# Attention and a gated MLP on one core: a score block split off, an eviction moved from ScalarE to VectorE, longer exponentials in the planner, new due times

## The chip, the cores and the metric

The kernel runs on one core of a Trainium2 chip. The metric is the device time of one execution in microseconds (us). The kernel before took 622.55 us, the median of three runs (621.22 to 623.7). The engines are named as in the profile: PE is TensorE's matmul stream and PEld its weight loads, DVE is VectorE, ACT is ScalarE, POOL is GpSimd, and SP is the queue that issues every DMA of this kernel.

## The reference, cut to what matters

```
q, k, v: (4, 12, 448, 64)                  # batch, heads, sequence, head size
scores = q @ k.T / 8, causal mask          # 448 x 448 a head
attn   = exp(scores - rowmax); attn /= sum(attn) + 1e-9
x      = (attn @ v), heads side by side    # (1792, 768)
gate   = 1 / (1 + exp(-(x @ w_gate)))      # 768 -> 1536
val    = x @ w_val
out    = (gate * val) @ w_out              # (1792, 768), float32
```

All inputs and the output are float32; the weights arrive in a packed 64-bit form.

## The kernel before, in words

The 48 heads are worked on as 24 pairs, two heads beside each other on the 128 partitions (six pairs for each of the four batch items). The six pairs of batch item 0 are the opening, and nothing but attention can run there at first, since the MLP needs their result. From then on the MLP of earlier batch items fills PE while the attention of later ones goes on beside it.

For one pair of the opening, the score rows are cut in four blocks of 128, 256, 384 and 448 keys (the last one has 64 rows and holds both heads together). `score` puts the products of blocks 0 and 1 in one step, block 2 in a second and block 3 in a third; blocks 0 and 1 of a head share a PSUM buffer. `softmax` then issues, block by block, a VectorE instruction that adds the mask, scales, and keeps the row's minimum of the negated scores (line 410); a ScalarE exponential with a running sum (line 417); two small VectorE instructions for the reciprocal (lines 426, 428); and GpSimd multiplications (line 438). `trans` turns the result on PE in four groups of four 128 x 128 tiles (line 313), and `empty` copies each group out of PSUM, on ScalarE for the groups listed in `EV` (line 322) and on VectorE for the others (line 324). `pv` multiplies with the values (lines 337, 342). From pair 6 on ("wide" pairs) the transposes are made on VectorE and through DRAM instead: `shift` writes the tile `tb` to DRAM as `pd` (line 461) and reads it back in four quarters as `pt` (line 464), and `wpv` (line 481) needs all four and the values `vr` (line 285).

The scores' inputs `raw` (line 274) and an extra piece in `sm` (line 279) are loaded for every pair; pair 0's `raw` comes in two pieces. The packed weights come in as `room` (line 559), are unpacked by ScalarE (line 563) and VectorE (lines 565, 567), stored as `wdram` for later use (line 570), and split in a high and a low part (lines 575, 577), so that each float32 product is three matmuls (lines 594, 807).

The order in which the instructions are written out is not the order of the Python calls. `Plan` notes each piece of work as an operation with an engine, an estimated cost, what it reads and writes, and a due time; operations are numbered as they are noted. `order` works the due times back from consumers to producers (consumer's due time less its cost, less a slack, less an extra of some operations, which for DMA loads is their latency), adds `NUDGE[number]` to single operations, and then plays the engines forward: each engine takes, of the operations that are ready, the one with the earliest due time. The instructions are written out in the order of these planned starts, and each engine and the SP queue then work strictly in that order; on the chip only semaphores hold an instruction back. A load must also follow the load before it in the same ring of buffers. The estimated cost of an exponential of n elements is `act(n, 0, 1) + 0.01`, which is n/1200 + 0.20 us.

Operation numbers that the prediction speaks of, as they count in the changed kernel: 40 is the `raw` load of pair 1, 41 its `sm` piece and 42 the values of pair 0; 253 and 261 are the loads of the first two packed weights (252 and 260 before); 814 is the `pd` store and 815 the first `pt` quarter for the wide pair whose value products come at 162.59 us; 820 to 842 are parts of the softmax of the next wide pair, 883 a GpSimd instruction of the MLP (line 624), 908 that pair's values, and 929 the store of an output tile (line 641). The base due times named there are those that the planner works out for the kernel before, ahead of `NUDGE`.

Of the kernel before, what the change touches and what calls it, by code (L numbers as in the profile page):

```python
# [20 lines left out]
NB = 4  # L21
# [14 lines left out]
AHEAD = 3  # L36
EARLY = 2
WC = 512
EV = (1, 3)
BUFS = dict(w64=3, wd=2, wr=3, ws=3, sm=4, raw=3, pt=2, gt=5, vr=2, st=4, tb=1)  # L40
LAT, LOOK, SLACK = 0.04, 0.06, 0.2
AFTER = dict(DVE=0.09, ACT=0.1, PL=0.03)
# [3 lines left out]
REBIAS, SIGN = 2.0 ** -112, 2.0 ** 32  # L46

NUDGE = {
# [7 lines left out]
}  # L56


# [149 lines left out]
def kernel(  # L208
# [7 lines left out]
    nc = tc.nc  # L216
    plan = Plan()
# [9 lines left out]
    act = lambda n, psum=0, acc=0: n / 1200 + (0.06 if psum else 0.09) + 0.1 * acc  # L227
# [3 lines left out]
    mask = new("mask", [128, ZM + WQ + HALF], F32)  # L231
# [56 lines left out]
    def score(n, blocks, due):  # L288

        j = pairs[n]  # L290
        if blocks[0] == 0:
            for k in ("mn", "sum", "r"):
                j[k] = new(k, [128, 2, NB], F32, BUFS["st"])
            j["sp"] = {}
        tag = "m" if j["b"] == 0 and blocks[0] == 2 and j["k"] < 3 else "s"
        sp = [new(tag, [128, 512], F32, 3, PSUM) for z in range(2)]
        j["sp"].update({i: (sp, woff(i) - woff(blocks[0])) for i in blocks})
        needs = [(j["raw"], *((0,) if blocks[-1] == 1 else (0, 1)))] + ([(j["sm"][1], "x")] if blocks[-1] == 3 else [])
        burst((qk_cost(blocks), lambda: products(j, blocks), needs, [(p,) for p in sp]), due)
        return lambda: softmax(j, blocks)  # L300

    def trans(n, g, due):
# [16 lines left out]
    def empty(j, g, tp):  # L319
        pt, o = j["pt"], 4 * WQ * g  # L320
        if g in EV:
            plan.op("ACT", act(4 * WQ, 1), lambda: nc.scalar.copy(pt.t[:, o:o + 4 * WQ], tp.t), [(tp,)], [(pt, g)])
# [37 lines left out]
    qk_cost = lambda blocks: sum(keys(i) / 600 if i < 3 else 0.4 for i in blocks) + 0.19  # L360
# [28 lines left out]
    def wscore(n, due):  # L389
        j = pairs[n]  # L390
        for k in ("mn", "sum", "r"):
            j[k] = new(k, [128, 2, NB], F32, BUFS["st"])
        a, b = ([new(tag, [128, 512], F32, bufs, PSUM) for z in range(2)] for tag, bufs in (("s", 3), ("t", 2)))
        j["sp"] = {0: (a, 384), 1: (b, 0), 2: (a, 0), 3: (b, 256)}
        burst((1.95, lambda: products(j, range(NB)), [(j["raw"], 0, 1), (j["sm"][1], "x")], [(p,) for p in a + b]), due)
        return lambda: softmax(j, range(NB))

    def softmax(j, blocks):
        mn, su, r_ = j["mn"], j["sum"], j["r"]
        for i in blocks:  # L400
            last = i == 3
            heads = range(1 if last else 2)
            sp, o = j["sp"][i]
            ne, off = keys(i), woff(i)
            for z in range(2):
                sm, n = j["sm"][0 if last else z], HALF if last else ne
                f, lo = (off + HALF * z, (ZM + WQ) * z) if last else (off, ZM - i * WQ)
                to = 1 - z if last else z
                first = lambda z=z, i=i, last=last: mn.t[:, 1, i:i + 1] if last and z else 3.0e38
                plan.op("DVE", dve(n), lambda z=z, i=i, sp=sp, sm=sm, n=n, o=o, f=f, lo=lo, to=to, first=first: nc.vector.tensor_tensor_reduce(  # L410
                    out=sm.t[:, f:f + n], in0=sp[z].t[:, o:o + n], in1=mask.t[:, lo:lo + n], scale=-0.125, scalar=first(),
                    op0=ALU.add, op1=ALU.min, accum_out=mn.t[:, to, i:i + 1],
                ), [(sp[z],), (mask, "end") if last and z else (mask,)] + ([(mn, (1, i))] if last and z else []),
                    [(sm, (i, z) if last else i), (mn, (to, i))])
            for z in heads:
                sm = j["sm"][z]
                plan.op("ACT", act(ne, 0, 1) + 0.01, lambda z=z, sm=sm, i=i, ne=ne, off=off: nc.scalar.activation(  # L417
                    out=sm.t[:, off:off + ne], in_=sm.t[:, off:off + ne], func=ACTF.Exp, scale=-1.0,
                    bias=mn.t[:, z, i:i + 1], accum_out=su.t[:, z, i:i + 1],
                ), [(mn, (z, i))], [*([(sm, (i, 0), (i, 1))] if last else []), (sm, i), (su, (z, i))], extra=0.1)  # L420
            if i < 2:
                continue
            group = (3,) if last else (0, 1, 2)
            a = slice(group[0], group[-1] + 1)
            h = slice(0, len(heads))
            plan.op("DVE", 0.13, lambda h=h, a=a: nc.vector.tensor_scalar_add(r_.t[:, h, a], su.t[:, h, a], 1e-9),
                    [(su, *[(z, e) for z in heads for e in group])], [(r_, last)])
            plan.op("DVE", 0.11, lambda h=h, a=a: nc.vector.reciprocal(r_.t[:, h, a], r_.t[:, h, a]), [], [(r_, last)])  # L428
            for z in heads:
                sm = j["sm"][z]  # L430
                for e in group:
                    o, w = woff(e), keys(e)
                    if j["b"] == 0 and j["k"] == HP - 1 and e % 2:
                        plan.op("ACT", act(w) + 0.1, lambda sm=sm, e=e, o=o, w=w, z=z: nc.scalar.activation(
                            out=sm.t[:, o:o + w], in_=sm.t[:, o:o + w], func=ACTF.Copy, scale=r_.t[:, z, e:e + 1]),
                            [(r_, last)], [(sm, e)])
                    else:
                        plan.op("PL", 0.24 + w / 1200, lambda sm=sm, e=e, o=o, w=w, z=z: nc.gpsimd.tensor_scalar(  # L438
                            out=sm.t[:, o:o + w], in0=sm.t[:, o:o + w], scalar1=r_.t[:, z, e:e + 1], scalar2=1.0,
                            op0=ALU.mult, op1=ALU.mult), [(r_, last)], [(sm, e)])  # L440
# [48 lines left out]
    def burst(part, due):  # L489
        held.append(part)  # L490
# [519 lines left out]
    last = [PAIR * HP + k for k in range(HP)] + [(PAIR + 1) * HP + k for i in range(KH) for k in (i, KH + i)]  # L1010
# [84 lines left out]
```

## Time and profile before

| what | before |
|---|---|
| median of three runs | 622.55 us |
| the profiled execution's own time | 620.8 us |
| its span, first to last instruction | 619.1 us |
| PE busy | 606.9 us (98%) |
| DVE busy | 439.7 us (71%) |
| ACT busy | 335.6 us (54%) |
| POOL busy | 310.6 us (50%) |

Busy time of an engine counts its own instructions; matmuls overlap in the array, so a busy PE is a PE that was never empty and not one at its peak. The profiled execution took 1.75 us less than the median of the runs; the sums are made against its own time.

### The profile page before, as it was taken

The numbers are of one execution on the slowest core, as the hardware profiler recorded it, in microseconds if no ns is written. First come the engines' busy times: TensorE is split into PE (matmuls) and PEld (weight loads), VectorE is DVE, ScalarE is ACT, GpSimd is POOL, SyncE is SP. The second block draws the span as 40 slices with busy tenths as digits, with TensorE's granted clock in tenths as the row PEclk, the third lists the DMA queues.
The fourth block names the chain that finished last, engine by engine and source line by source line (L and its number), as shares of the span: only waits on it lengthen the run. The fifth ranks groups of instructions, "written<-read, shape, count | busy, mean of one in ns | idle before, by whom it ended". The sixth has DMA issues, their size and how long they took to land.

```text
span 619.1 us, 11867 instructions
## 1 busy us (share of the span) xinstructions
PE 606.9 (98%) x4182; PEld 531.5 (86%) x4182; DVE 439.7 (71%) x1048; ACT 335.6 (54%) x754; POOL 310.6 (50%) x350
## 2 busy tenths in 40 slices
PE   6999999999999999999999999999999999999997
PEld 3578888898888888888888899989999989999996
DVE  5897999889855546544648766577754688999752
ACT  6996765675634755555558644434333443657420
POOL 5650534614300676767676676658664666611200
PEclk9999999999999999999999999999999999999999
DMA  8688999998999999878786886855533213534321
GB/s 299 203 308 314 344 370 378 376 397 320 364 396 339 321 365 344 293 245 319 269 323 247 281 311 238 276 199 189 179 110 95 77 52 103 159 117 142 112 75 60
DMA packets 54348, 153.35 MB, mean 248 GB/s; under 512 B 6032, under 2 KB 12432, under 8 KB 51984
## 3 DMA queue, kind: packets, MB, share of 16 engines
q1 hardware_dynamic: 54288, 152.59, 69.6%
q8 instruction: 33, 0.54, 0.3%
q14 instruction: 27, 0.22, 0.1%
HBM read 109.31 MB, written 43.25 MB: 246 GB/s over the span
## 4 chain that ended last, share of the span: by engine, by line
PE 89%; DMA 4%; DVE 3%; ACT 2%; issue 1%; POOL 0%; SPq 0%; DVEq 0%; ACTq 0%; POOLq 0%
PE m L594 39%; PE m L807 19%; PE s L807 10%; PE t L807 7%; PE m L481 5%; PE s L387 4%; PE t L387 2%; DMA raw<-in_qkt_dram 2%; DMA pd<-tb 1%; DMA vr<-in_vt_dram 1%; PE t L313 1%; ACT sm L417 1%; DVE wr L567 1%; DVE sm L410 1%; POOL sm L438 0%
## 5 line engine op out<-in xcount | busy, mean ns | idle before, releaser
L761 POOL TENSOR_TENSOR wl<-room,wh 128x384 fp32r<-128x384 f32 x84 | 98.0, 1190 | 56.0 <-ACT wh L760 56.0
L438 POOL TENSOR_SCALAR sm<-sm,r 128x384 f32<-128x384 f32 (+3 forms) x165 | 94.1, 591 | 63.6 <-DVE r L428 50.2
L594 PE MATMUL m<-xh,wh 128*128 128x448 f32 x288 | 107.3, 372 | 0.0
L594 PE MATMUL m<-xh,wl 128*128 128x448 f32 x288 | 105.3, 366 | 0.0
L594 PE MATMUL m<-xl,wh 128*128 128x448 f32 x288 | 105.2, 365 | 0.0
L417 ACT ACTIVATE sm<-sm,mn 128x384 f32<-128x384 f32 (+3 forms) x168 | 87.6, 524 | 18.6 <-DVE mn L410 15.2
L577 POOL TENSOR_TENSOR wl<-wr,wh 128x768 fp32r<-128x768 f32 x38 | 70.6, 1872 | 24.1 <-ACT wh L575 20.8
L575 ACT CAST wh<-wr 128x768 fp32r<-128x768 f32 x72 | 59.8, 832 | 33.4 <-DVE wr L567 15.0
L760 ACT CAST wh<-room 128x384 fp32r<-128x384 f32 x84 | 39.8, 511 | 52.5 <-PE s L807 12.7
L410 DVE CUSTOM_DVE_ANT_0 sm<-s,mask 128x128 f32<-128x128 f32 (+3 forms) x108 | 42.5, 408 | 25.8 <-PE s L387 25.7
L594 PEld LDWEIGHTS m<-xh,wh 128*128 128x128 f32 x288 | 54.1, 188 | 6.6 <-issue 1.6
L594 PEld LDWEIGHTS m<-xh,wl 128*128 128x128 f32 x288 | 54.1, 188 | 4.5
L594 PEld LDWEIGHTS m<-xl,wh 128*128 128x128 f32 x288 | 54.1, 188 | 4.1
L594 PE MATMUL m<-gh,wh 128*128 128x448 f32 x144 | 53.3, 370 | 0.0
L594 PE MATMUL m<-gh,wl 128*128 128x448 f32 x144 | 52.6, 365 | 0.0
L594 PE MATMUL m<-gl,wh 128*128 128x448 f32 x144 | 52.6, 365 | 0.0
L624 POOL TENSOR_TENSOR gl<-gt,gh 128x448 fp32r<-128x448 f32 x24 | 28.9, 1208 | 37.4 <-ACT gh L623 27.3
L807 PE MATMUL m<-pt,wh 128*128 128x448 f32 x150 | 44.8, 367 | 0.2 <-DVE xl L676 0.2
L453 DVE STREAM_TRANSPOSE room<-sm 128x384 f32<-128x384 f32 (+2 forms) x84 | 35.4, 449 | 8.8 <-POOL sm L438 8.4
L387 PE MATMUL s<-raw 64*64 64x128 f32 (+3 forms) x432 | 35.7, 390 | 4.6 <-DMA raw<-in_qkt_dram 3.5
L481 PEld LDWEIGHTS m<-pt,vr 128*64 128x64 f32 x720 | 33.5, 137 | 7.8 <-issue 4.3
L577 DVE TENSOR_TENSOR wl<-wr,wh 128x768 fp32r<-128x768 f32 x34 | 33.5, 984 | 7.9 <-ACT wh L575 7.4
(177 smaller groups left out, 1373.7 us busy)
## 6 DMA issues: line engine op xcount, KB each, us to landing
room<-in_wp_dram SPq DMA_DIRECT2D x36, 768.0 KB, 7.4
pt<-pd SPq DMA_DIRECT2D x72, 256.0 KB, 5.6
wr<-wdram SPq DMA_DIRECT2D x45, 384.0 KB, 4.6
room<-wdram SPq DMA_DIRECT2D x45, 384.0 KB, 3.6
wdram<-wr SPq DMA_DIRECT2D x36, 384.0 KB, 7.6
pd<-room SPq DMA_DIRECT2D x12, 1024.0 KB, 4.7
raw<-in_qkt_dram SPq DMA_DIRECT2D x23, 448.0 KB, 5.9
vr<-in_vt_dram SPq DMA_DIRECT2D x24, 256.0 KB, 5.3
```

Source lines behind the costliest of these rows:

```text
L387: nc.tensor.matmul(out=sp[z].t[c:c + 64, o:o + ne], lhsT=q, rhs=k)
L410: plan.op("DVE", dve(n), lambda z=z, i=i, sp=sp, sm=sm, n=n, o=o, f=f, lo=lo, to=to, first=first: nc.vector.tensor_tensor_reduce(out=sm.t[ ...
L417: plan.op("ACT", act(ne, 0, 1) + 0.01, lambda z=z, sm=sm, i=i, ne=ne, off=off: nc.scalar.activation(out=sm.t[:, off:off + ne], in_=sm.t[:, ...
L438: plan.op("PL", 0.24 + w / 1200, lambda sm=sm, e=e, o=o, w=w, z=z: nc.gpsimd.tensor_scalar(out=sm.t[:, o:o + w], in0=sm.t[:, o:o + w], sca ...
L453: plan.op("DVE", dve(128 * c) + 0.03, lambda sm=sm, i=i, o=o, c=c, at=at: nc.vector.transpose(out=tv()[:, :, at:at + 32 * c].rearrange("p ...
L481: nc.tensor.matmul(out=vp.t[64 * z:64 * z + 64, i * WQ:i * WQ + rows(i)], lhsT=v.t[:, c, z], rhs=src, start=(c == 0), stop=(c == i))
L575: plan.op("ACT", act(768), lambda: nc.scalar.copy(hi_.t, t.t), [(t,)], [(hi_,)])
L577: plan.op(eng, cost, lambda: at.tensor_tensor(out=lo_.t, in0=t.t, in1=hi_.t.bitcast(F32), op=ALU.subtract), [(t,), (hi_,)], [(lo_,)], lock ...
L594: nc.tensor.matmul(out=ps.t[:, :S], lhsT=a.t[:, k, :], rhs=b.t if isinstance(b, Buf) else b(), start=(first and z == 0), stop=(last and z ...
L760: plan.op("ACT", act(w), lambda: nc.scalar.copy(f(hi_.t), x()), [(src, at)], [(hi_, e)])
L761: plan.op("PL", 0.97, lambda: nc.gpsimd.tensor_tensor(out=f(lo_.t), in0=x(), in1=f(hi_.t).bitcast(F32), op=ALU.subtract), [(src, at), (hi_ ...
L807: nc.tensor.matmul(out=ps.t[:, :S], lhsT=a.t[:, kw, :], rhs=b.at, start=bool(first and z == 0), stop=bool(last and z == 2), skip_group_che ...
```

## The change

Five things change. `EV` loses group 3, so the last of the four transposed groups of each opening pair is copied out of PSUM by VectorE and no longer by ScalarE. In `score`, for the first pair alone (n < 1), the step of blocks 0 and 1 becomes two steps, and block 0 is due 0.3 us ahead of block 1. The dependency of `softmax` on the products is now noted by block instead of by buffer. The planner's cost of an exponential rises by 0.08 us. And `NUDGE` is replaced as a whole; since the first pair has one operation more, all operation numbers from 11 on mean the operation that had a number one lower before.

```diff
-EV = (1, 3)
+EV = (1,)
 NUDGE = {
-    12: -0.9, 31: -3.1, 100: -1.6, 108: -1.6, 144: -3.4, 180: 2.5, 181: 2.5, 187: -3.1, 252: -9.6, 260: -9.6,
...
-    808: 3.4, 811: 3.4, 813: 3.3, 822: -0.2, 835: 0.7, 836: 0.7, 837: 0.7, 838: 9.1, 840: 2, 907: -0.9,
-    928: -8.4, 957: -2.6, 984: 3.2, 1055: -3.7, 1064: -2.4, 1065: -2.4, 1072: 0.5, 1076: -2.4, 1077: -2.4,
...
+    40: 5.9, 49: -4.4, 151: -6.3, 156: -4.1, 157: -4.1, 159: 8.5, 166: 4.9, 263: 2.8, 282: -1.9, 316: 1.7,
...
+    469: -0.5, 472: 13.1, 508: 1.1, 525: -4.3, 648: 4.5, 652: 5, 695: 1.1, 701: -0.7, 815: 3, 820: -16.2,
+    823: -4.7, 826: -4.7, 827: -4.7, 830: -4.7, 831: -4.7, 842: -4.7, 883: 2.1, 921: 1.6, 929: 18, 934: -1.6,
...
 }
...
-        burst((qk_cost(blocks), lambda: products(j, blocks), needs, [(p,) for p in sp]), due)
+        if n < 1 and len(blocks) > 1:
+            for i in blocks[:-1]:
+                plan.op("PE", qk_cost((i,)), lambda i=i: products(j, (i,)), needs, [(p, i) for p in sp], due - 0.3)
+        here = blocks[-1:] if n < 1 else blocks
+        burst((qk_cost(here), lambda: products(j, here), needs, [(p, *here) for p in sp]), due)
...
-                ), [(sp[z],), (mask, "end") if last and z else (mask,)] + ([(mn, (1, i))] if last and z else []),
+                ), [(sp[z], i), (mask, "end") if last and z else (mask,)] + ([(mn, (1, i))] if last and z else []),
...
-                plan.op("ACT", act(ne, 0, 1) + 0.01, lambda z=z, sm=sm, i=i, ne=ne, off=off: nc.scalar.activation(
+                plan.op("ACT", act(ne, 0, 1) + 0.09, lambda z=z, sm=sm, i=i, ne=ne, off=off: nc.scalar.activation(
```

## Rows read from the trace of the kernel before

**Rows 1.** The page's first part: busy us, share of the span, instructions.
```profile
PE 606.9 (98%) x4182; PEld 531.5 (86%) x4182; DVE 439.7 (71%) x1048; ACT 335.6 (54%) x754; POOL 310.6 (50%) x350
```

**Rows 2.** Waits of PE, whole span: us in total, times, longest us.
```profile
PE s L387 <- DMA raw<-in_qkt_dram: 3.5, 1, 3.5
PE m L481 <- DMA vr<-in_vt_dram: 1.8, 2, 1.2
PE t L313 <- POOL sm L438: 0.7, 1, 0.7
PE s L387 <- DVE mn L410: 0.6, 1, 0.6
PE s L387 <- DVE r L426: 0.5, 1, 0.5
PE m L387 <- DMA raw<-in_qkt_dram: 0.5, 1, 0.5
PE t L313 <- DVE pt L324: 0.3, 1, 0.3
PE m L807 <- DVE xl L676: 0.2, 1, 0.2
```

**Rows 3.** Stages: us, then busy us (instructions) of each engine, PEclk, DMA share, GB/s.
```profile
5.00:47.00 42.00, 38.99 (x411) 25.75 (x404) 37.76 (x147) 38.44 (x111) 24.77 (x41) 1.00 0.82 284
...
150.00:200.00 50.00, 48.21 (x318) 43.57 (x320) 34.23 (x61) 25.21 (x42) 5.68 (x11) 1.00 1.01 372
200.00:604.00 404.00, 403.73 (x2594) 361.79 (x2587) 272.07 (x612) 202.11 (x456) 236.93 (x236) 1.00 0.61 209
604.00:619.10 15.10, 11.44 (x57) 10.26 (x55) 3.52 (x6) 0.84 (x1) 0.00 (x0) 1.00 0.17 61
```

**Rows 4.** Timeline of the start: start us, us, instruction [idle before, releaser].
```profile
3.47 1.56 PE L387 MATMUL s<-raw 64*64 64x128 f32 x16 [3.47 <-DMA raw<-in_qkt_dram]
...
5.20 0.29 DVE L410 CUSTOM_DVE_ANT_0 sm<-s,mask 128x128 f32<-128x128 f32 x1 [5.20 <-PE s L387]
```

**Rows 5.** Timeline of the SP queue, first 7 us: when each DMA is issued.
```profile
2.18 0.43 SPq L274 DMA_DIRECT2D raw<-in_qkt_dram  x1
2.66 0.43 SPq L279 DMA_DIRECT2D sm<-in_qkt_dram  x1
3.13 0.43 SPq L285 DMA_DIRECT2D vr<-in_vt_dram  x1
...
4.08 1.15 SPq L559 DMA_DIRECT2D room<-in_wp_dram  x2
...
6.87 3.74 SPq L274 DMA_DIRECT2D raw<-in_qkt_dram  x2
```

**Rows 6.** DMA issues of those windows: KB each, us from issue to landing.
```profile
raw<-in_qkt_dram SPq DMA_DIRECT2D x1, 448.0 KB, 5.1
sm<-in_qkt_dram SPq DMA_DIRECT2D x1, 144.0 KB, 5.0
vr<-in_vt_dram SPq DMA_DIRECT2D x1, 256.0 KB, 5.5
```

**Rows 7.** The two copies of the opening, 5 to 41 us: ns min/median/max.
```profile
L322 ACT COPY pt<-t x9: 562/567/610, 13.4 to 40.0; 128x512 f32<-128x512 f32 x9
L324 DVE COPY pt<-t x9: 674/687/693, 11.7 to 38.2; 128x512 f32<-128x512 f32 x9
```

**Rows 8.** Timeline of ACT: two exponentials that follow each other.
```profile
29.59 0.39 ACT L417 ACTIVATE sm<-sm,mn 128x128 f32<-128x128 f32 x1
29.98 0.39 ACT L417 ACTIVATE sm<-sm,mn 128x128 f32<-128x128 f32 x1
```

**Rows 9.** Timelines of SP, ACT and POOL, 145 to 159 us.
```profile
145.34 0.36 SPq L461 DMA_DIRECT2D pd<-tb  x1
...
157.90 0.89 ACT L563 ACTIVATE wd<-room 128x768 f32<-128x768 f32 x1
...
157.08 1.61 POOL L624 TENSOR_TENSOR gl<-gt,gh 128x448 fp32r<-128x448 f32 x1 [3.62 <-ACT gh L623]
```

More of the change, by code (lines that the diff above doesn't have):

```diff
@@ L394, in wscore @@
         j["sp"] = {0: (a, 384), 1: (b, 0), 2: (a, 0), 3: (b, 256)}
-        burst((1.95, lambda: products(j, range(NB)), [(j["raw"], 0, 1), (j["sm"][1], "x")], [(p,) for p in a + b]), due)
+        burst((1.95, lambda: products(j, range(NB)), [(j["raw"], 0, 1), (j["sm"][1], "x")], [(p, 0, 2) for p in a] + [(p, 1, 3) for p in b]), due)
         return lambda: softmax(j, range(NB))
```

8 rows, old and new, of the table NUDGE are left out of this document.

## The prediction, written before the changed kernel was run

> **What bounds the kernel now.** The page's first part comes first: PE is busy for 606.9 of 619.1 us and no other engine for more than 439.7 [rows 1]. The number and shapes of the matmuls do not change, so the change can only act on the 12.2 us in which PE was empty. The waits of PE say where these lie: 3.5 us until the first input, two waits of together 1.8 us for the values of wide pairs, and then six of 0.7 us and less, five of them in the opening [rows 2]. The windows by stage confirm it: from 200 to 604 us PE lacks 404.00 - 403.73 = 0.27 us, from 150 to 200 us it lacks 1.79, and in the opening, from 5 to 47 us, it lacks 42.00 - 38.99 = 3.01; the 3.66 that it lacks after 604 us are the last output's way out, which the change leaves alone [rows 3]. The reader should take two things from these rows. A speed-up of more than about 1% is not there to be had, and the two places that count are the opening and the two waits near 162 and 180 us. The opening is also the one stage where PE is not alone: ACT is busy for 38.44 and DVE for 37.76 of the 42 us [rows 3], so that all three are above 89%.
>
> Half a per cent, 3.1 us, is about what a measurement of this kernel can tell from no change. That is more than the whole idle time of PE in the opening.
>
> **The change, part by part.** The sum is made against the profiled execution, 620.8 us; the median of the runs is 1.75 us above it, and I add that at the end.
>
> *The split of the first score block: 0 us, between -1.0 and 0.* Before, the 16 matmuls of blocks 0 and 1 run from 3.47 to 5.03 us and DVE starts on block 0 at 5.20, 0.17 after the last of them [rows 4]. Block 1 has twice the columns of block 0, so about two thirds of the 1.56 us are block 1's, and if block 0 alone released DVE, it would start some 1.0 us earlier and all that follows with it. That is the -1.0. I take 0, since the planner lets block 1 start the moment block 0 ends (PE has nothing else then) and plans DVE's first instruction 0.04 us later (its `LAT`), so both product steps are still written out ahead of the read, and both write one PSUM buffer. The trace has a wait for the end of both; it does not say whether the wait goes by the buffer or by the columns.
> The Trainium skill (PSUM — Partial Sum Buffer, section "PSUM bank collisions raise a hardware error") has the rule that semaphores should guard PSUM by bank and quadrant and not by address, as a read beside a write in other columns of the bank already collides. By that rule the read of block 0 has to wait for block 1 and the split is worth nothing; by columns it would be worth the 1.0 us. The trace's 5.20 us agrees with the rule, but a single step would look like this either way.
>
> *The `raw` load of pair 1 goes back: +0.6 us, between 0 and +1.4.* Operation 40 has a base due time of 2.8 and gets +5.9, so 8.7. The `sm` piece (5.1) and the values of pair 0 (6.4) are earlier and now go ahead of it on SP; pair 2's `raw` (8.3) cannot, as it must follow 40 in its ring. The landings give the price: the three were issued at 2.18, 2.66 and 3.13 us [rows 5] and took 5.1, 5.0 and 5.5 us [rows 6], so they landed at 7.3, 7.7 and 8.6. They land one after the other. With `raw` as the last of the three, it lands at about 8.6 and not at 7.3: 1.4 us, rounded with what the issue costs. PE waited for it already (0.5 us, its only wait for `raw` after the first [rows 2]), so that wait becomes 1.9. But behind it PE waited 0.5 us for a DVE instruction and then for GpSimd's multiplications of pair 0, which this load doesn't delay [rows 2]; these waits shrink as PE comes later. If they swallow the delay it costs nothing, if ACT's stream simply starts 1.4 later it costs 1.4. I take a bit under half. In the same move the two 768 KB weight loads lose their -9.6; they were issued at 4.08, ahead of a `raw` that was issued at 6.87 [rows 5], and now go behind it. That helps pair 3's input, which nobody waited for [rows 2], and costs nothing, as the first weights are used 30 us later.
>
> *Group 3's copy on DVE, and the exponentials' true cost: -0.8 us, between -2.1 and +2.1.* Six pairs, one copy each. ACT loses 6 x 0.567 = 3.4 us and DVE gains 6 x 0.687 = 4.1 us [rows 7]. DVE has 42.00 - 37.76 = 4.24 us idle in the opening and ACT 3.56 [rows 3]: after it DVE is busy for 41.9 of 42 us and ACT for 35. By busy time alone the load is not balanced but handed over. For a gain speaks that PE's waits in the opening after the first name POOL (0.7), DVE (0.6, 0.5, 0.3) [rows 2], all of them at the end of a chain through the exponentials, and that the planner so far believed the exponentials too short: 128 elements count as 0.307 us there and come every 0.39 us on the chip [rows 8], 0.08 us each and seven of them a pair, 0.56 us a pair that the plan did not see. With the true cost the written order fits ACT's real pace. If all four waits go the gain is 0.7 + 0.6 + 0.5 + 0.3 = 2.1. The loss is 2.1 if DVE can use half of its idle time for the copies. Between ends that lie alike I take -0.8: the unpacking of the first two weights (lines 565, 567) now comes later, where DVE has room.
>
> *The two waits for values: -1.6 us, between -1.8 and +1.0.* These are wide pairs, and the chain runs from softmax through `pd`, `pt` and `vr` to PE, one DMA after the other. For the first, the store `pd` was nudged by +3.3 and two of the transposes ahead of it by +3.4; these nudges are gone, so `pd` (base 137.0) is now due ahead of a weight store (139.1) and a weight load (138.0) that stood before it. The core's DMA moves 372 GB/s here with a share of 1.01 [rows 3], so a 384 KB store is 1.06 us, a 768 KB load twice that: `pd`, issued at 145.34 before [rows 9], can go up to 3 us earlier, and the wait is 1.2 us [rows 2]. Against it, operation 815 sends one `pt` quarter behind a 384 KB store: 1.06 us back, the +1.0 at the upper end. For the second, exponentials get -4.7 and so pass a 0.89 us unpacking that ran at 157.90 between them; a 1.61 us POOL instruction ahead of the multiplications gets +2.1 [rows 9], and an output store +18. Together 2 to 3 us off a chain that was late by the rest of the 1.8. It loses 1.06, as `vr` lost its -0.9 and falls behind a store. That leaves both waits closed, less 0.2 that I keep for a remainder.
>
> *The late wait:* 0.2 us for DVE's `xl` [rows 2]; the copies ahead of it get -2.4 and -2.8. -0.2, between that and 0.
>
> *All other due times: +0.4 us, between 0 and +1.8.* About sixty single due times are new and as many old ones, which may each have closed a wait, are gone. The windows show 0.27 us of idle PE in 404 us [rows 3], so nothing is left to gain there and only something to lose. A new wait in a wide pair would be of the size of the two seen, 1.8; I take a quarter of it.
>
> The sum: 0 + 0.6 - 0.8 - 1.6 - 0.2 + 0.4 = -1.6 us. The profiled execution would take 619.2, the median of the runs 622.55 - 1.6 = 620.95, so 621.0.
>
> **The rivals.**
> *Nearly all waits close.* The split frees DVE (-1.0), the late `raw` is swallowed (0), the opening gains 2.1, both value waits go (-1.8) and nothing new comes: with -0.2, -5.1 us, 617.5. For it speaks that every large wait in [rows 2] has a due time near it that moves the right way; against it, operation 40, which makes a wait longer, and DVE's 41.9 of 42 us.
> *DVE becomes the bound of the opening.* 4.1 us are put on an engine with 4.24 us idle. If none of that idle time can be used (it is idle while PE's products are not there), the opening is longer by 4.1; with the late `raw` at its worst (1.4) and the rest as forecast (-1.6 - 0.2 + 0.4) this is +4.1, 626.7. It decides, as a slowdown of over 3.1 us, once less than 1.0 us of the idle time can be used. Against it speaks that PE's and DVE's waits are spread over all pairs, so that some of it will do.
> *The change does not do what it says.* The split waits as before, the copies change places beside other work, and waits that go come back at the next buffer: within 0.5 us of before, 622.5.
>
> **How the numbers follow.** The forecast (619.4 to 622.6) has 0.50, the closing of nearly all waits 0.22, DVE as the bound 0.13, and no effect 0.15. Faster by over 0.5% (below 619.4) holds the second and a lower tail of the first, 0.26; slower by over 0.5% (above 625.7) is the third, 0.13; the rest, 0.61, is within. The range from 617.6 to 624.6 cuts off half of the second case and nearly all of the third, about 2 in 10.
>
> **What would show it.** Right: PE's 1.8 us for `vr` gone from its waits; its second wait for `raw` near 1.9 us and not 0.5; in the window from 5 to 47 us ACT near 35 and DVE near 41 us busy; DVE's first line-410 instruction still after both blocks' products, near 5.2. Wrong: PE's busy time in 200 to 604 us falling by more than 1 us; a PE wait for line 324 or 410 of over 1 us in the opening; or the first DVE instruction near 4.3 us.

## The result and the profile after

The changed kernel is slower: 626.79 us, median of five runs (624.80 to 627.57; a sixth execution took 1211 us for a reason that no trace shows and is left out), beside 621.29 us for the kernel before, median of six measured with it (620.13 to 623.70). The ratio is 1.0074, with an interval of 1.0051 to 1.0097 (the two medians by themselves make 1.0089). The forecast was 621.0 with a range up to 624.6, so it fell on the wrong side. The profiled execution took 624.8 us with a span of 623.1, against 620.8 and 619.1 before: 4.0 us to account for. It is the quickest of the five, and no trace shows what the others had beyond it.

PE has the same 4182 matmuls, 1.5 us more busy time, and less work on ACT, as the page's first part says:

```profile
PE 608.4 (98%) x4182; PEld 532.8 (86%) x4182; DVE 441.3 (71%) x1054; ACT 332.0 (53%) x748; POOL 309.0 (50%) x350
```

The waits of PE over the whole span (us in total, times, longest us) have changed their names. The 1.8 us for `vr` of [rows 2] are gone, as forecast, but 2.6 us for `pt` stand in their place, and two late waits of 0.7 and 0.6 us are new:

```profile
PE s L391 <- DMA raw<-in_qkt_dram: 3.7, 1, 3.7
PE m L485 <- DMA pt<-pd: 2.6, 1, 2.6
PE t L317 <- POOL sm L442: 1.5, 5, 0.4
PE s L391 <- DVE mn L414: 1.2, 1, 1.2
PE m L485 <- DMA out_dram<-gt: 0.7, 1, 0.7
PE t L811 <- ACT xh L838: 0.6, 1, 0.6
```

The windows by stage, with the columns of [rows 3] (busy us of PE, PEld, DVE, ACT, POOL; granted clock; DMA share; GB/s), say where to look. PE's idle time from 5 to 47 us is 42.00 - 38.52 = 3.48 us (3.01 before), from 150 to 200 us 2.58 (1.79 before), from 200 to 604 us 1.35 (0.27 before). And the granted clock is no longer 1.00 in the second of these:

```profile
5.00:47.00 42.00, 38.52 (x406) 24.68 (x398) 37.36 (x149) 34.53 (x104) 25.67 (x41) 1.00 0.80 275
...
150.00:200.00 50.00, 47.42 (x286) 43.65 (x285) 34.60 (x62) 25.96 (x43) 8.24 (x12) 0.97 0.96 336
200.00:604.00 404.00, 402.65 (x2608) 360.84 (x2607) 271.17 (x610) 201.39 (x456) 234.30 (x236) 1.00 0.62 211
```

The value products of the second of the two wide pairs of [rows 2] ("the second wide pair" from here on), in PE's timeline (start, duration, idle before them and what ended it), hold most of the loss. First the kernel before, then the changed one:

```profile
179.94 2.00 PE L481 MATMUL m<-pt,vr 128*64 128x128 f32 x40 [0.56 <-DMA vr<-in_vt_dram]
```

```profile
181.75 3.63 PE L485 MATMUL m<-pt,vr 128*64 128x128 f32 x40 [2.58 <-DMA pt<-pd]
```

PE waits 2.0 us longer, and then the same 40 matmuls take 3.63 us and not 2.00. Windows of PE alone, for the changed kernel, show why: with the wait the granted clock drops from its upper level (2.4 GHz) to its lower one (1.2 GHz) for a while.

```profile
175.00:180.00 5.00, 4.18 (x21) 1.00 1.02 305
180.00:185.00 5.00, 3.25 (x37) 0.68 0.98 377
185.00:190.00 5.00, 5.00 (x32) 0.98 1.00 369
```

The lower level is half of the upper one, so a mean of 0.68 over 5 us means that 3.2 us of them were at it (5 - 0.5 x 3.2 = 3.4 = 0.68 x 5), and 0.98 in the next window 0.2 more.

Where the wait comes from is read on the SP queue. Before, and then after (start, duration of the issue, and what was issued):

```profile
163.77 0.32 SPq L461 DMA_DIRECT2D pd<-tb  x1
165.21 0.33 SPq L559 DMA_DIRECT2D room<-in_wp_dram  x1
```

```profile
164.05 0.33 SPq L563 DMA_DIRECT2D room<-in_wp_dram  x1
164.47 0.38 SPq L465 DMA_DIRECT2D pd<-tb  x1
```

The two have changed places. The chain of waits of either kernel gives the price, as the piece in which the chain stood on the `pd` transfer (start, us, what):

```profile
163.77 6.49 DMA pd<-tb
```

```profile
164.47 9.13 DMA pd<-tb
```

The store landed at 173.60 and not at 170.26, and the `pt` quarters that read it back could only be issued then. The 3.34 us have three parts. The tile `tb` was complete later, at 164.20 and not at 163.75; the load then stood ahead, so the store was issued 0.27 us after that and not 0.02; and it was 2.64 us longer on its way. The first part was meant to be a gain, and the engines' timelines show where the gain went. Before (the last instruction that writes `tb`, and GpSimd's multiplications ahead of it):

```profile
159.77 3.36 POOL L438 TENSOR_SCALAR sm<-sm,r 128x256 f32<-128x256 f32 x7 [1.08 <-DVE r L428]
163.17 0.58 DVE L453 STREAM_TRANSPOSE tb<-sm 128x384 f32<-128x384 f32 x1
```

After:

```profile
156.43 3.80 POOL L442 TENSOR_SCALAR sm<-sm,r 128x384 f32<-128x384 f32 x5 [5.20 <-PE m L598]
160.20 1.16 POOL L628 TENSOR_TENSOR gl<-gt,gh 128x448 fp32r<-128x448 f32 x1
161.33 1.81 POOL L442 TENSOR_SCALAR sm<-sm,r 128x128 f32<-128x128 f32 x2
162.83 0.31 DVE L457 STREAM_TRANSPOSE tb<-sm 128x128 f32<-128x128 f32 x1 [0.19 <-POOL sm L442]
163.07 0.92 DVE L571 SCALAR_TENSOR_TENSOR wr<-room,wr 128x768 int32<-128x768 int32 x1
163.90 0.30 DVE L457 STREAM_TRANSPOSE tb<-sm 128x128 f32<-128x128 f32 x1
```

The multiplications start 3.3 us earlier, as the earlier exponentials were meant to make them, and still end at the same time, 163.1 us. The MLP instruction that was moved away from the place ahead of them now stands in their middle, and four of the seven take about twice as long as before (the two of 128x256 1.04 us each and not 0.48, the two of 128x128 0.92 and not 0.37) while VectorE unpacks and splits weights beside them; no run tells whether that is the reason. Then the last transpose into `tb` stands behind an unpacking of 0.92 us on VectorE. That same unpacking (line 571) had to end before the load could be issued, as it frees the load's buffer: the load went out at 164.05, just before `tb` was complete.

In the plan the load is due at 154.6 and the store (operation 918) at 154.9. These 0.3 us are the same in the kernel before. There, however, the planner has the load ready only at 168.8, after the store's planned start at 168.2; in the changed kernel it has the load ready at 164.6 and the store at 164.9, both ahead of the queue's next free moment at 167.5, and then the due time decides.

A ledger of the profiled execution, by the start of value products that both kernels have. At the end of the opening these are, before and after:

```profile
47.26 1.52 PE L337 MATMUL s<-pt,vr 128*64 128x384 f32 x12
```

```profile
48.37 1.51 PE L341 MATMUL s<-pt,vr 128*64 128x384 f32 x12
```

| stretch | PE later than before by | of it new |
|---|---|---|
| end of the opening, 47 us | +1.1 | +1.1 (0.2 of it the first input; two more traces with the same order of the opening have +0.8 and +2.15) |
| first wide value products, 162 us | -0.2 | -1.3: the first wait, 1.23 us, is closed |
| second, 182 us | +1.8 | +2.0: the longer wait |
| a pair further, 224 us | +3.5 | +1.65: the lower clock |
| last matmul, 615 us | +4.0 | +0.6: two late waits of 1.35 in all, less small gains |

### The profile page after: what moved, and what is told of

Its sections match the earlier page's. It is cut to its first block, busy times and chain, and to the rows that moved or that the text cites. A ratio compares the mean times of both kernels' runs of the same rounds, so it can differ in the third digit from the quotient of the medians.

```text
span 623.1 us, 11866 instructions
## 1 busy us (share of the span) xinstructions
PE 608.4 (98%) x4182; PEld 532.8 (86%) x4182; DVE 441.3 (71%) x1054; ACT 332.0 (53%) x748; POOL 309.0 (50%) x350
## 4 chain that ended last, share of the span: by engine, by line
PE 89%; DMA 4%; DVE 3%; POOL 2%; ACT 1%; issue 0%; SPq 0%; DVEq 0%; POOLq 0%
PE m L598 38%; PE m L811 19%; PE s L811 11%; PE t L811 7%; PE m L485 6%; PE s L391 4%; PE t L391 2%; POOL sm L442 2%; DMA pd<-tb 1%; DVE sm L414 1%; DMA pt<-pd 1%; DVE pt L328 1%; PE t L317 1%; DMA out_dram<-gt 1%; DVE wr L571 1%; ACT sm L421 0%
## 5 line engine op out<-in xcount | busy, mean ns | idle before, releaser
L765 POOL TENSOR_TENSOR wl<-room,wh 128x384 fp32r<-128x384 f32 x84 | 96.3, 1167 | 59.1 <-ACT wh L764 56.0
L421 ACT ACTIVATE sm<-sm,mn 128x256 f32<-128x256 f32 (+3 forms) x168 | 87.5, 524 | 15.7 <-DVE mn L414 15.1
L485 PEld LDWEIGHTS m<-pt,vr 128*64 128x64 f32 x720 | 35.1, 142 | 9.2 <-issue 7.5
L485 PE MATMUL m<-pt,vr 128*64 128x128 f32 (+1 forms) x720 | 37.6, 262 | 3.3 <-DMA pt<-pd 2.6
```

Source lines behind the costliest of these rows:

```text
L421: plan.op("ACT", act(ne, 0, 1) + 0.09, lambda z=z, sm=sm, i=i, ne=ne, off=off: nc.scalar.activation(out=sm.t[:, off:off + ne], in_=sm.t[:, ...
L485: nc.tensor.matmul(out=vp.t[64 * z:64 * z + 64, i * WQ:i * WQ + rows(i)], lhsT=v.t[:, c, z], rhs=src, start=(c == 0), stop=(c == i))
L765: plan.op("PL", 0.97, lambda: nc.gpsimd.tensor_tensor(out=f(lo_.t), in0=x(), in1=f(hi_.t).bitcast(F32), op=ALU.subtract), [(src, at), (hi_ ...
```

## The experiments

The theory (A): the new due times put a weight load ahead of the wide pair's store; the wait that follows, and the lower clock after it, are the loss. The rivals: (B) the copies and the late `raw` load make the opening longer, and (C) many small waits. Each kernel ran 5 to 12 times, beside the kernel before on the same chip. The expectations count PE's waits some 0.15 us longer than its timeline does (1.39 us for 1.23, 2.07 for 1.91); the text goes by the timeline.

**One due time.** The changed kernel with the store due half a microsecond earlier.

```diff
 NUDGE = {
...
+    918: -0.5,
```

> The changed kernel with one due time more: 918: -0.5, so that the `pd` store of the last wide pair of the first half (issued at 164.47 us, landed at 173.60) goes out ahead of the weight load that was issued at 164.05. Theory A (this order is the loss: the wait of 2.6 us for `pt` at 181.75 and the 3.4 us at half clock that followed it in the changed kernel's trace): `pd` lands about 4 us earlier, the wait goes, the granted clock stays at 1.00 from 150 to 200 us, and the time falls by 2.6 + 1.7 = 4.3 us, to within 1 us of the kernel before. Rival B (the opening: the later `raw` load and the copies on VectorE): only the wait moves, the time falls by less than 1 us. Rival C (many new due times, each a little): a fall of 1 to 2.5 us.

622.33 us, ratio 1.0017 (1.0001 to 1.0033), where the change has 1.0074: three quarters of the loss is gone, by one store that goes 0.55 us earlier and ahead of one load. By the planner nothing else moves but four further places on the SP queue and three on ScalarE, all behind this one; PE's, VectorE's and GpSimd's orders are those of the change. The chain of waits, PE's timeline, and PE's window:

```profile
163.92 4.88 DMA pd<-tb
```

```profile
179.76 2.00 PE L485 MATMUL m<-pt,vr 128*64 128x128 f32 x40 [0.89 <-DMA pt<-pd]
```

```profile
180.00:185.00 5.00, 5.00 (x56) 1.00 1.02 421
```

The store now takes 4.88 us and not 9.13. The load ahead of it moves 768 KB, which at the 372 GB/s of [rows 3] is 2.1 us; the other half of the difference of 4.25 us is not accounted for by it, and I leave it open.

**The order before, with a load of the same size in the way.** The kernel before, with an extra 768 KB load (nobody reads it) issued ahead of that store, once and twice. The diff is that of one; the second kernel has a 2 in place of the 1.

```diff
-        plan.op("SP", dma(128 * 4 * WC * 4), lambda: nc.sync.dma_start(out=pd.t, in_=at_()),
+        more = [new(f"extra{e}", [128, 2 * DM], I32, 1, bass.MemoryType.DRAM) for e in range(1 * (n == 11))]
+
+        def store():
+            for e, x in enumerate(more):
+                x.make()
+                nc.sync.dma_start(out=x.t, in_=wp[e])
+            nc.sync.dma_start(out=pd.t, in_=at_())
+
+        plan.op("SP", dma(128 * 4 * WC * 4), store,
```

> The kernel before, in every engine's order, with one extra 768 KB DMA (packed weights to a scratch buffer in DRAM) issued just ahead of the same pair's `pd` store; its result is not used. Theory A: `pd`, `pt` and `vr` land about 2 us later, PE's wait of 0.7 us near 180 becomes about 2.8, the clock falls to one half for some 3.4 us behind it, and the kernel before becomes slower by 2.1 us for the wait and about 1.7 for the clock, 3 to 4 us in all. If a wait costs its own length alone: 2 us. Rivals B and C: nothing here speaks against them unless the time does not change at all.

One load: 622.13 us, ratio 1.0016 (1.0002 to 1.0030). The store landed 2.5 us later, but `vr`, which PE waits for, only 0.6 us later, as the four `pt` quarters ahead of it were issued in 1.77 us and not 3.03 and it was itself 5.77 us on its way and not 6.39. PE's wait was 1.18 us and the clock stayed up. The expectation of 3 to 4 us was missed: of the store's delay of 2.5 us only 0.6 reached the last load of the chain.

```profile
180.47 2.00 PE L489 MATMUL m<-pt,vr 128*64 128x128 f32 x40 [1.18 <-DMA vr<-in_vt_dram]
```

> The kernel before with two extra 768 KB DMAs to scratch ahead of the same `pd` store (one of them made `vr` land only 0.6 us later and PE's wait 1.33 us long, for +0.9 us; the clock stayed full). Theory A: the pair's wait on PE grows to about 3.5 us, longer than the 2.6 us of the changed kernel, and is followed by some 3 us at half clock, about 1.7 us on top: PE is 2.8 + 1.7 = 4.5 us behind the kernel before from there on. If the half clock had another cause, PE is 2.8 us behind and the clock is full until PE's last matmul.

Two loads: 626.40 us, ratio 1.0076 (1.0063 to 1.0089), a loss as large as the change's with nothing of the change in it (its wait is longer, its opening is that of the kernel before). PE's timeline and windows:

```profile
183.93 3.68 PE L489 MATMUL m<-pt,vr 128*64 128x128 f32 x40 [3.77 <-DMA vr<-in_vt_dram]
```

```profile
180.00:185.00 5.00, 1.23 (x11) 0.78 0.99 373
185.00:190.00 5.00, 5.00 (x42) 0.54 1.03 419
```

So a late store at this place is enough for a loss of this size, and the lower clock comes with the wait, whatever order of instructions led to it.

**The copies alone, and the split alone.** The kernel before with the third copy on VectorE; and, in a second kernel, with the split and the finer dependencies and nothing else (the old due times stay on the operations that they belonged to).

```diff
-EV = (1, 3)
+EV = (1,)
```

> The kernel before with EV = (1,) alone: six copies out of PSUM go from ScalarE (0.567 us each) to VectorE (0.687), planned with the old costs and due times. Rival B (VectorE becomes the bound of the opening): +1.5 to +4 us, with PE's idle time from 5 to 47 us well over the 3.0 of before and VectorE near 42 us busy. Theory A: the copies find idle time, within 1 us of before.

623.15 us, ratio 1.0031 (1.0016 to 1.0045): a loss of its own, and not the small gain of the forecast. PE reaches 47 us of the opening 1.26 us later, though its busy time from 5 to 47 us is 38.98 us, 0.01 from that of [rows 3], and the second wide pair's value products 2.4 us later. Four further traces with the opening of the kernel before, or with the split alone, lie within 0.3 us of it at 47 us.

```diff
...
-        burst((qk_cost(blocks), lambda: products(j, blocks), needs, [(p,) for p in sp]), due)
+        if n < 1 and len(blocks) > 1:
+            for i in blocks[:-1]:
+                plan.op("PE", qk_cost((i,)), lambda i=i: products(j, (i,)), needs, [(p, i) for p in sp], due - 0.3)
+        here = blocks[-1:] if n < 1 else blocks
+        burst((qk_cost(here), lambda: products(j, here), needs, [(p, *here) for p in sp]), due)
...
```

> The kernel before with the split of the first score block alone (old `EV`, old cost of an exponential, the old due times on the operations that they belonged to). The split leaves PE's, ScalarE's, GpSimd's and SP's order as it was and exchanges two VectorE instructions. All theories: VectorE's first instruction of line 410 still starts 0.17 us after the products of both blocks, and the time is that of before within 0.5 us. If the split released VectorE by block, it would start about 1.0 us earlier.

621.66 us, ratio 1.0003 (0.9991 to 1.0014): no change. The copies with the longer exponentials, and the longer exponentials alone, were not run.

**The late `raw` load.** The change without `40: 5.9`.

```diff
 NUDGE = {
-    40: 5.9, 49: -4.4, 151: -6.3, 156: -4.1, 157: -4.1, 159: 8.5, 166: 4.9, 263: 2.8, 282: -1.9, 316: 1.7,
...
+    49: -4.4, 151: -6.3, 156: -4.1, 157: -4.1, 159: 8.5, 166: 4.9, 263: 2.8, 282: -1.9, 316: 1.7, 382: 1.7,
...
```

> The changed kernel without 40: 5.9, so that pair 1's `raw` load goes ahead of the `sm` piece and the values again; everything else, the late `pd` too, as in the changed kernel. The prediction's term: +0.6 us for the late load, so 0.6 less (0 to 1.3): `raw` lands at 7.3 us and not at 8.5, PE's wait of 1.25 us there is about 0.5. If the waits behind it swallow it, the time does not change.

624.45 us, ratio 1.0055 (1.0043 to 1.0067), an interval that overlaps the change's (1.0051 to 1.0097). PE reached 47 us 0.57 us sooner than in the change, as expected, and then waited longer for the same `pt` quarter (3.47 us beside 2.58). But the three traces with `40: 5.9`, whose opening is written in one and the same order, stand at +0.8, +1.1 and +2.15 us at 47 us beside the kernel before, and the three without it that have VectorE's copies at +0.5, +0.9 and +1.2. The 0.57 is less than what one order scatters by, so the price of the late `raw` load stays open.

**The two late waits.** The change without `2566: 3.2`, and with the weight load that stood ahead of the `pt` quarters near 371 us ordered behind them.

```diff
 NUDGE = {
...
-    1109: -6.2, 1123: -0.3, 1207: -1.5, 1217: 2.7, 1249: 9.9, 1505: -13.8, 1524: 3.4, 1599: 2.2, 1601: 2.2,
-    1979: -2.8, 1981: -2.4, 1982: -2.4, 2309: 1.5, 2566: 3.2, 2647: 7.4, 2718: 3.2,
+    1109: -6.2, 1123: -0.3, 1207: -1.5, 1217: 2.7, 1249: 9.9, 1505: -13.8, 1524: 3.4, 1599: 2.2, 1601: 2.2, 1979: -2.8,
+    1981: -2.4, 1982: -2.4, 2309: 1.5, 2647: 7.4, 2718: 3.2,
 }
...
+        self.behind(self.ops[2248], self.ops[1941])
```

> The changed kernel with two late waits taken away: without 2566: 3.2 (the PE step that this nudge set right behind the operation that it depends on through a PSUM buffer, wait of 0.79 us at 509.40), and with the weight reload 2248 ordered behind the four `pt` quarters of the last pair (it was issued at 370.51, waiting for GpSimd, and the quarters stood behind it; wait of 0.88 us at 377.96). Theory C's share: both waits go and the time falls by 1.2 to 1.7 us. If they are only shifted to the next DMA: 0.

623.26 us, ratio 1.0049 (1.0031 to 1.0068); beside the change's 1.0074 that is some 1.5 us, about what the two waits are together (0.72 and 0.63 us), but the two intervals overlap, so the size isn't shown. Both waits are gone from PE's list, and that much is. For the first of them the changed kernel's list names an output store. The SP queue shows the four quarters, issued at 366.17 us in the kernel before, standing behind a weight load that could only be issued at 370.51:

```profile
370.51 0.32 SPq L738 DMA_DIRECT2D wr<-wdram  x1
370.92 1.86 SPq L468 DMA_DIRECT2D pt<-pd  x4
```

The kernel's own profiled execution took 626.3 us, the second slowest of its seven (622.4 to 626.3): its opening was later and its `pt` wait was 4.09 us. So its trace doesn't give the size either.

**All three together,** `918: -0.5`, without `40: 5.9`, and with the two late waits mended.

> The changed kernel with the `pd` store ahead of the weight load (918: -0.5), without 40 and 2566 and with 2248 behind the quarters. If the four places are the whole loss but the copies: 1.0 (from the run with the `pd` store ahead, 622.3 against 621.4) less 0.5 for `raw` and less 1.4 for the late waits, so about 0.9 us under the kernel before, 620.5. If the copies on VectorE still cost the opening 1.3 us as they did alone, the PE milestones stay 0.3 to 0.8 us behind there and the time is that of before.

620.55 us, ratio 0.9988 (0.9973 to 1.0004): the loss is gone and no gain is left. The third copy on VectorE and the later opening (1.16 us later than before at 47 us) are still in it, so rival B is no loss that has to stay. Rival C is confined to the two late waits, whose price is not clear of the noise. PE still waits 1.91 us at the second wide pair, and the clock stays up:

```profile
181.15 2.00 PE L486 MATMUL m<-pt,vr 128*64 128x128 f32 x40 [1.91 <-DMA pt<-pd]
```

**That wait closed too.** As the last, with the second wide pair's values due 8 us earlier and its nudged `pt` quarter (921) set back to its base time.

```diff
 NUDGE = {
...
-    826: -4.7, 827: -4.7, 830: -4.7, 831: -4.7, 842: -4.7, 883: 2.1, 918: -0.5, 921: 1.6, 929: 18, 934: -1.6,
+    826: -4.7, 827: -4.7, 830: -4.7, 831: -4.7, 842: -4.7, 883: 2.1, 908: -8, 918: -0.5, 929: 18, 934: -1.6,
...
```

> The kernel with all four places mended, and the last quarter's chain shortened: the values of that pair go out ahead of the `pd` store (908: -8) and the first quarter loses its +1.6, so that neither stands behind the 384 KB store that went between the quarters (last quarter landed at 181.01, two places and 2.2 us behind the third). Expected from theory A: PE's wait of 2.07 us at 181.15 goes, the clock was full there already, so the time falls by about 2 us, to 618.6. If another DMA takes its place in the queue: no change.

618.88 us, ratio 0.9969 (0.9958 to 0.9981): faster than either kernel. From 150 to 200 us and from 200 to 604 us PE has no gap:

```profile
150.00:200.00 50.00, 50.00 (x330) 1.00 0.99 360
```

```profile
200.00:604.00 404.00, 404.00 (x2595) 363.46 (x2594) 270.99 (x610) 202.64 (x455) 235.47 (x236) 1.00 0.61 209
```

**The copy put back on ScalarE** in the kernel with all three mended.

```diff
-EV = (1,)
+EV = (1, 3)
```

> The kernel with all four places mended (620.55 against 620.93 of the kernel before), with EV = (1, 3) again: group 3's copies back on ScalarE, the rest of the changed kernel kept. If the copies cost the opening 1.3 us here as they did alone in the kernel before (PE's milestones +1.3 us from 47 us on), the time falls by 1 to 1.5 us, to about 619.3. If, with the true cost of the exponentials in the plan, the copies are free on VectorE: no change, or up to 1 us slower, as ScalarE has 3.4 us more to do.

623.22 us, ratio 1.0030 (1.0014 to 1.0046), slower than with the copy on VectorE. But the planner's order moved with it, and the second wide pair waited again. In its profiled execution:

```profile
182.63 3.56 PE L486 MATMUL m<-pt,vr 128*64 128x128 f32 x40 [2.21 <-DMA pt<-pd]
```

Six of its twelve runs have a mean granted clock of 0.999 or 1.0 and took 621.0 to 622.7 us; the other six have 0.995 to 0.997 and took 623.7 to 626.0. Whether the wait itself was longer in these six no trace shows.

**The old due times.** First the kernel before without the three nudges ahead of the first wide store, and then the change's structure (split, copies, cost) with the due times of the kernel before.

```diff
 NUDGE = {
...
-    808: 3.4, 811: 3.4, 813: 3.3, 822: -0.2, 835: 0.7, 836: 0.7, 837: 0.7, 838: 9.1, 840: 2, 907: -0.9,
...
+    822: -0.2, 835: 0.7, 836: 0.7, 837: 0.7, 838: 9.1, 840: 2, 907: -0.9, 928: -8.4, 957: -2.6, 984: 3.2,
...
```

> The kernel before without 808, 811 and 813 (three due times of the first of the two wide pairs that PE waits for). The prediction's step for this pair said that `pd` goes ahead of a weight store and a weight load and the wait of 1.39 us at 162.59 closes. By the plan's order `pd` passes the store alone. If that is enough the time falls by up to 1.4 us; the changed kernel did close this wait, but may owe it to the exponentials' cost and to the order of the values. If not: the wait stays and the time is that of before.

621.47 us, ratio 1.0008 (0.9995 to 1.0021): no change; the first wait was 1.46 us, not closed, and the second wide pair had no wait in this trace.

```diff
 NUDGE = {
-    40: 5.9, 49: -4.4, 151: -6.3, 156: -4.1, 157: -4.1, 159: 8.5, 166: 4.9, 263: 2.8, 282: -1.9, 316: 1.7,
...
+    13: -0.9, 32: -3.1, 101: -1.6, 109: -1.6, 145: -3.4, 181: 2.5, 182: 2.5, 188: -3.1, 253: -9.6, 261: -9.6,
...
```

> The changed kernel with the due times of the kernel before on the operations that they belonged to: split, copies on VectorE and longer exponentials are in, the new due times are not. If the new due times are the whole loss (theory A), the time is that of before or within 2 us of it, since the copies alone cost 1.9. If the structure is the loss whatever the due times are, it is as slow as the changed kernel, 625 to 627. The two waits near 162 and 180 us tell which: the plan puts `pd` behind three weight transfers here.

626.39 us, ratio 1.0084 (1.0070 to 1.0097): as slow as the change. PE's waits (as above) and its timeline:

```profile
PE s L390 <- DMA raw<-in_qkt_dram: 3.6, 1, 3.6
PE m L484 <- DMA vr<-in_vt_dram: 2.8, 1, 2.8
PE t L316 <- POOL sm L441: 2.0, 5, 0.6
PE m L597 <- DVE wl L580: 0.8, 1, 0.8
```

```profile
167.25 2.55 PE L484 MATMUL m<-pt,vr 128*64 128x128 f32 x40 [2.76 <-DMA vr<-in_vt_dram]
```

So theory A falls in its strong form: the new due times as such are not the loss. Without them the rest of the change (split, copies, longer exponentials) leads to an order that has its long wait at the first wide pair; the new due times close that one and open the other. Which of the three does it isn't shown: the split alone costs nothing, the copies alone cost 1.9 us, and the exponentials' cost was not changed by itself. What holds in all these kernels is the narrower form: where a wide pair's transfers land late for PE's value products, PE waits, and in these traces the waits of 2.21 us and more cost more than themselves, those of up to 1.91 us did not.

The waits at the second wide pair (at the first where it says so) and the duration of the 40 value products behind them, each from PE's timeline as above, in the order of the wait:

| kernel | wait, us | 40 products, us |
|---|---|---|
| split alone; before without three nudges; that wait closed too | 0 | 2.00 |
| before | 0.56 | 2.00 |
| store 0.5 earlier | 0.89 | 2.00 |
| one extra load | 1.18 | 2.00 |
| copies alone | 1.55 | 2.00 |
| all three mended | 1.91 | 2.00 |
| copy put back | 2.21 | 3.56 |
| the change | 2.58 | 3.63 |
| old due times (first wide pair) | 2.76 | 2.55 |
| without `40: 5.9` | 3.47 | 3.35 |
| two extra loads | 3.77 | 3.68 |
| late waits mended | 4.09 | 3.68 |

## Why the prediction was wrong, point by point

**The step that failed is "the two waits for values: -1.6 us", in its second half.** The exponentials, the POOL instruction and the output store moved away were to take "2 to 3 us off a chain that was late", and that "leaves both waits closed". The runs show the chain not shortened but longer. The exponentials did what was asked (GpSimd's multiplications start 3.3 us earlier), but the work that was moved stands in the middle of the chain and no longer ahead of it, the multiplications beside it took 5.6 us and not 3.4, and `tb` was complete 0.45 us later. On the queue the step looked at `vr` alone: the store `pd` got no nudge and I didn't place it. Its neighbour, a 768 KB load, became ready 4 us earlier in the plan and went ahead of it, and the store landed 3.3 us later. The wait of 0.56 us became 2.58, where it was forecast to close.

Its first half came out: the first wait, 1.23 us, is gone, and that pair's `pd` was issued at 142.84 us and not at 145.34, ahead of the weight load and the weight store, 2.5 us of the "up to 3 us" given. The reason given is not enough for it: with the three nudges taken out of the kernel before, `pd` was issued at 145.65 and the wait stayed, at 1.46 us. Which other part of the change does the rest is open.

**The price of the wait was not in the sum at all.** Every wait was put at its own length. Behind this one came 1.65 us at the lower clock, nearly as much as the wait had grown. The experiments show the pair together: +2.0 and +1.65 us with the late store, +0.3 us and a clock at its upper level with the store ahead of the load. The clock isn't the larger part: one run of the change has a mean granted clock of 1.0 and still took 625.31 us, and two runs with two extra loads have 0.999 and 1.0 and took 624.83 and 625.18; no trace of these exists.

**"Group 3's copy on DVE, and the exponentials' true cost: -0.8"** had the wrong sign as well, though its size stays uncertain. With the `raw` term (+0.6) the opening was forecast at -0.2 and came out at +1.1. The copies alone were +1.26 at the end of the opening and 1.0031 in the run. The mechanism feared for it isn't there: DVE was busy for 37.36 us from 5 to 47 us, not the 41 I gave as a sign, since four more copies came into the stretch (+2.6 us) while two of the five unpackings of line 567 (now 571), and some of the other work, went out of it; ACT's 34.53 is as forecast. What shows is a shift of PE's waits: those for POOL go from one of 0.7 us to five of together 1.5, and with the copies alone to three of together 1.4. As the copy put back gave no gain either (its opening stood at +1.7), I can't say that VectorE is the wrong engine for it.

**"The `raw` load of pair 1 goes back: +0.6"** is neither confirmed nor refuted. One pair of traces has 0.57, less than the openings of one order scatter by. The sign named for it (PE's wait for `raw` near 1.9) came as 1.25 us before the same products. The profile names a VectorE instruction there, but that `raw`, issued at 3.13 us and 5.4 us on its way, landed only about 0.1 us before they start:

```profile
8.66 0.88 PE L391 MATMUL s<-raw 64*64 64x128 f32 x16 [1.25 <-DVE mn L414]
```

**"The split: 0"** is right. DVE starts on block 0 at 5.39 us, 0.17 us after the last product of both blocks, as in [rows 4], and the split alone is 1.0003:

```profile
3.66 1.56 PE L391 MATMUL s<-raw 64*64 64x128 f32 x16 [3.66 <-DMA raw<-in_qkt_dram]
...
5.39 0.29 DVE L414 CUSTOM_DVE_ANT_0 sm<-s,mask 128x128 f32<-128x128 f32 x1 [5.39 <-PE s L391]
```

The Trainium skill (PSUM — Partial Sum Buffer, section "PSUM bank collisions raise a hardware error") wants semaphores to guard PSUM by bank and quadrant; the trace's 0.17 us agrees with that, as the read waited for the other block of its buffer.

**"The late wait: -0.2" and "all other due times: +0.4":** the wait for `xl` is gone, and two new ones of 0.72 and 0.63 us stand in its place. PE lacks 1.35 us from 200 to 604 us and not 0.27, so the two terms together are +1.1 us by the profiled execution where +0.2 was forecast: too small, but within the +1.8 that was allowed. The reason held: there was nothing to gain from 200 to 604 us and something to lose.

**The signs.** Two of the three signs of being wrong came: PE's busy time from 200 to 604 us fell by 1.08 us (403.73 to 402.65), and in the opening stands the wait of 1.25 us above, which the profile puts down to what was line 410. Of the signs of being right, "PE's 1.8 us for `vr` gone from its waits" came too, and says nothing, as the wait came back under the name of `pt`.

**The rivals.** "DVE becomes the bound of the opening" gave 626.7, almost the measured 626.79, by a mechanism that the trace refutes (37.36 us of 42): that the number fits is luck. The right rival, a store passed by a load on the queue, was not among them, though the same text did the sum for `vr` and for one `pt` quarter.

**What stays open:** 2 us of the store's 9.13 that the load's size doesn't explain; why four multiplications took twice as long; the 2 us by which the median run of the change is above the profiled one; what the longer exponentials do alone; and what of the opening belongs to the copies and what to the order that the planner makes of them.

## What to carry to other kernels

When a change re-times a plan, follow the whole chain to the late consumer on its queue too, operation by operation, with the moment at which it and its neighbours become ready and not its due time alone: here a 768 KB load that became ready earlier went ahead of a store by 0.3 us of due time that had always been there, and half a microsecond on that one due time took three quarters of the loss away. Read off the trace too whether a chain that was to be shortened did end earlier: here its start moved by 3.3 us and its end did not. Compare a wait on the matmul engine with waits of that engine elsewhere in the traces before putting it at its own length, as the long ones here came with a stretch of lower clock. And when a structural edit goes into a planner, time it alone with the due times left as they were, since these belong to the order that they were found for.

## What the runs showed of the hardware that was not expected

In the middle of a kernel, with PE busy before and after, a single wait of PE of up to 1.91 us left the granted clock at its upper level in the traces here, and every single one of 2.21 us and more came with a stretch at the lower one (the table above); between them lies no trace, and each kernel has one. The executions without a trace are less sharp. In the kernel at 2.21 us only half of the runs show the lower clock in their mean, and some 2.8 us lie between the medians of the two halves (624.3 and 621.4 us). The kernel before, whose traced waits are 1.23 and 0.56 us, has a mean clock of 0.995 to 0.997 in 9 of its 72 runs beside the experiments (median 623.3 us; 621.2 for the others), while the kernel at 1.91 us has none in 11. From the second wide pair's value products to those of the next wide pair the change needs 46.13 us where the kernel before needs 44.48; the kernel with two extra loads 47.13. And one 768 KB transfer ahead of the store made PE's wait 0.6 us longer in the order before (0.56 to 1.18), two made it 3.2 longer (to 3.77), and the one that the change put there 1.7 (0.89 to 2.58): so the price of one transfer was not a fixed one, and what else stood in the queue differed.
